# K by eight heads and a quarter of the keys, K and V in one ring: a decode step of attention beside an MLP

## The chip, the cores and the metric

The kernel runs on one core of a Trainium2 chip. The metric is the device time of one execution in microseconds (us). Before the change it is 214.77 us, the median of three runs (214.66 to 214.85). The core has five engines that run on their own and meet at semaphores: TensorE (PE, matmuls; its weight loads are shown apart as PEld), VectorE (DVE), ScalarE (ACT), GpSimd (POOL) and SyncE (SP), which here issues nearly all transfers. Sixteen DMA engines move the data.

## What is computed

One token for each of four sequences goes through two branches that are added: attention over the last 2048 keys of a cache, and an MLP behind a small mixing step.

```python
def _A_ref(x, k_cache, v_cache, wq, wo):
    W = min(4096, max(256, Sk // 4))          # 2048 of the 8192 keys
    rep = Hq // Hkv                           # 32 query heads on 16 kv heads
    q = (x @ wq).reshape(B, Sq, Hq, Dh).transpose(0, 2, 1, 3)
    k = jnp.repeat(k_cache[:, :, Sk - W:, :], rep, axis=1)
    v = jnp.repeat(v_cache[:, :, Sk - W:, :], rep, axis=1)
    scores = jnp.einsum("bhqd,bhkd->bhqk", q, k) * (Dh ** -0.5)
    p = _softmax(scores, axis=-1)
    o = jnp.einsum("bhqk,bhkd->bhqd", p, v)
    return o.transpose(0, 2, 1, 3).reshape(B, Sq, Hq * Dh) @ wo

def _B_ref(x, w1, w2, w3, w4):
    h = _gelu(_layernorm(x, axis=-1) @ w1)
...
    x1 = x + hs
    h2 = _gelu(_layernorm(x1, axis=-1) @ w3) @ w4
    return x1 + h2

xn = _layernorm(x, axis=-1)
return x + _A_ref(xn, A_k_cache, A_v_cache, A_wq, A_wo) + _B_ref(xn, B_w1, B_w2, B_w3, B_w4)
```

B is 4, D 576, F 4608, the head size Dh 128; everything is bf16. `k_cache` and `v_cache` have the shape (4, 16, 8192, 128), so a head of one sequence is 2 MB, of which the last half MB is read. Together the windows of K and V are 67 MB; the weights are 21 MB more.

## The kernel before

The program is written as a list of operations for each engine. Each has a key, and an engine's operations are sorted by it; each names the operations or counts that it waits for. A transfer is an operation of SP (line 176), so the transfers go out in the order of their keys, and one that waits holds up all behind it. All of them share one queue.

**Transfers.** First come the weights wq, w2, w1, w3 and the remainder of w3. wq, w1 and w2 lie in the V ring, w3 in `regB`, which later holds transposed keys. Then K: a unit is one kv head `g` of all four sequences, 2 MB, and lies in one of four slots of the K ring (lines 230 to 236). Partition p = 4 i + b holds the keys 64 i to 64 i + 63 of sequence b, one run of 16 KB in memory; the outer dimension of the source is i, 32 long. Units 0 to 3 wait for nothing, unit g waits until the transposes of unit g - 4 are done. V has the same layout in a ring of its own, also four slots. V0 goes after K8 (`V0_AFTER`), the rest after K15; V4 and on wait for PV of four units before. wo goes between V3 and V4 into the K ring (`WO_AFTER`, line 242). The five parts of w4 come last, into the V ring.

**Scores.** A block is eight 128x128 transposes on TensorE into one bank of PSUM (`pe_T`, line 345), with a permuted identity `perm_k` that sorts the columns by sequence, and one copy to `ktbuf` by VectorE or ScalarE (`evac`, line 355: blocks 1, 4 and 7 of eight go to ScalarE). Eight blocks are one unit. Then `pe_SC` (line 361) multiplies: 16 matmuls a unit, each with the queries of one head and one sequence as weights (32 columns, zero but for two) and 512 keys as the moving operand, into the 32 partitions of that sequence. All 16 heads add up in the same four banks, since each head's queries stand in columns of their own. The TensorE code is a hardware loop of four passes, four units each. The scores of a unit come two blocks into the next one, over the end of a pass too: a dummy unit -1 stands at the start, and the last unit's scores behind the loop.

**Softmax.** VectorE takes the maximum of each partition (`rmax`), ScalarE writes the exponentials bank by bank (L398), VectorE turns each quarter in 32x32 blocks as soon as its exponential is there (L401), TensorE permutes (L402), and VectorE makes the weights `PTg` of a unit (L412).

**Output.** `pe_PV` (line 444) is 64 matmuls a unit with the V tile as weights and 8 columns of `PTg`; VectorE normalizes the result (L456). This loop also has four passes of four units. Then a turn (L474), 64 matmuls with wo (`pe_AO`, line 465), and the products with w4 part by part (`MO0` to `MO4`, line 557): `MO0` adds into the accumulator of wo, which is then copied (L553) and folded into the final one (`pe_fold`, L543), and the other parts go straight to the final one (88 matmuls, L543). Two copies (L570, L571) and two small transfers end the kernel.

Of the kernel before, what the change touches and what calls it, by code (L numbers as in the profile page):

```python
# [6 lines left out]
BF16 = mybir.dt.bfloat16  # L7
# [5 lines left out]
NKS = 4  # L13
NVS = 4
# [3 lines left out]
NIT = 4  # L18
ACT_EVAC = (1, 4, 7)
WO_AFTER = 3  # L20
V0_AFTER = 8
# [17 lines left out]
def bass_parallel_sum__sliding_block_cached__mixer_s_mlp__decode_kernel(  # L39
# [11 lines left out]
    NHB = 8 * G  # L51
# [10 lines left out]
    with ExitStack() as ctx:  # L62
        def sb(name, shape, dt):
            return ctx.enter_context(nc.sbuf_tensor(name, shape, dt))
# [4 lines left out]
        kring_t = sb("kring", [128, NKS * UE], BF16)  # L69
        vring_t = sb("vring", [128, NVS * UE], BF16)  # L70
        W3E = 4 * F + FH
        regB_t = sb("regB", [128, max(NKT * 1024, W3E)], BF16)
        kring = kring_t[:].rearrange("p (s t d) -> p s t d", s=NKS, t=NT)
        vring = vring_t[:].rearrange("p (s t d) -> p s t d", s=NVS, t=NT)
        ktbuf = regB_t[:, 0:NKT * 1024].rearrange("p (s n) -> p s n", s=NKT)
        kttile = regB_t[:, 0:NKT * 1024].rearrange("p (t b i) -> p t b i", b=B, i=32)
        w3main = regB_t[:, 0:4 * F].rearrange("p (r n) -> p r n", r=4)
        w3rag = regB_t[:, 4 * F:W3E]
        wqmain = vring_t[:, 0:4 * Hq * Dh].rearrange("p (r n) -> p r n", r=4)
        wqrag = vring_t[:, 4 * Hq * Dh:4 * Hq * Dh + Hq * Dh // 2]  # L80
        wo_sb = kring_t[:, 0:32 * D].rearrange("p (r n) -> p r n", r=32)
        _o = 4 * Hq * Dh + Hq * Dh // 2
        w1p = vring_t[:, _o:_o + 9 * HALF]
        _o += 9 * HALF
        w2p = vring_t[:, _o:_o + 9 * HALF]
        _o += 9 * HALF
        WQ_SLOTS = -(-_o // UE)
        assert WQ_SLOTS < NVS

# [17 lines left out]
        Qs = sb("Qs", [128, 4, B, 32], BF16)  # L107
        ident_bf = sb("ident_bf", [128, 128], BF16)
        perm_k = sb("perm_k", [128, 128], BF16)
# [48 lines left out]
        for nm, cnt in (("eb", 32), ("qs", 4), ("pg", 4), ("on", 4)):  # L158
            for k in range(cnt):
                S[(nm, k)] = sem(f"{nm}{k}")  # L160
# [37 lines left out]
        P(lambda e: e.memset(Qs[:, 3], 0.0), sig=("qs", 3), key=-95.8)  # L198

        def first_counts(e):  # L200
            for k in range(NTB):
                e.sem_inc(S[("eb", 32 - NTB + k)], 1)
                e.sem_inc(S[("on", k)], 1)
        P(first_counts, key=-95.7)
        P(lambda e: e.tensor_copy(out=perm_k[:].rearrange("p (b i) -> p b i", b=B), in_=ident_bf[:].rearrange("p (i b) -> p b i", b=B)),
          waits=["ident_bf"], sig="perm_k", key=-95.5)
# [23 lines left out]
        def kv_pairs(ring_t, slot, cache, g):  # L230
            return [(ring_t[:, slot * UE:(slot + 1) * UE],
                     cache[:, g, Sk - W:Sk, :].rearrange("b (i t) d -> i b (t d)", t=NT))]

        for g in range(G):
            ev_k.append(add_dma(kv_pairs(kring_t, g % NKS, A_k_cache, g), ("k", g % NKS),
                                [f"T{8 * (g - NKS) + 7}"] if g >= NKS else [], g))
        wo_wait = f"T{8 * (G - 2) + 7}"
        for g in range(G):
            kk = KS + g if g else V0_AFTER + 0.5
            w = [f"PV{g - NVS}"] if g >= NVS else (["hT"] if g < WQ_SLOTS else [])  # L240
            ev_v.append(add_dma(kv_pairs(vring_t, g % NVS, A_v_cache, g), ("v", g % NVS), w, kk))
            if g == WO_AFTER:
                ev_wo = add_dma([(kring_t[:, 0:32 * D], A_wo.rearrange("(p r) n -> p (r n)", r=32))],
                                "wo", [wo_wait], kk + 0.1)
        w4_src = B_w4.rearrange("(p r) n -> p r n", r=RT)
        w4_sb = vring_t[:, 0:RT * D].rearrange("p (t n) -> p t n", n=D)
        for n, (t0, t1_) in enumerate(W4P):
            lst = (t1_ * D - 1) // UE
            ev_w4.append(add_dma([(w4_sb[:, t0:t1_, :], w4_src[:, t0:t1_, :])], ("w4", n),
                                 [f"PV{max(g for g in range(G) if g % NVS == lst)}"], KS + G + 0.1 * n))  # L250
# [91 lines left out]
        add("pe", pe_zeroS, waits=["zeros_bf", "perm_k", "gelu2", "gelu_h", "qT", "x1nT", "x1"], sig="zeroS", key=-1)  # L342


        def pe_T(n):
            g, k = n // 8, n % 8

            def f(e):
                ins = None
                for t in range(8):  # L350
                    ins = e.transpose(tb[n % NTB][:, t, :], kring[:, g % NKS, 8 * k + t, :], perm_k[:])  # L351
                return ins
            return f
# [7 lines left out]
        def pe_SC(g):  # L361
            def f(e):
                ins = None
                for c4 in range(4):
                    for b in range(B):
                        t0 = 8 * ((8 * g + 2 * c4) % NKT)
                        ins = e.matmul(Sps[32 * b:32 * b + 32, c4, :].rearrange("p (t i) -> p t i", t=16), lhsT=Qs[:, g % 4, b, :],  # L367
                                       rhs=kttile[:, t0:t0 + 16, b, :],
                                       start=False, stop=(g == G - 1), tile_position=(0, 32 * b), skip_group_check=True)
                return ins  # L370
            return f

        for n in range(NHB):
            p = n % 32
            w = [("L", ("k", p // 8), 16)] if p % 8 == 0 else []
            w.append(("L", ("eb", (p - NTB) % 32), 1))
            add("pe", pe_T(n), waits=w, sig=f"T{n}", key=n // 32 + 0.01 * p, loop=("k", n // 32))
            eng, f = evac(n)
            add(eng, f, waits=[f"T{n}"] + ([f"SC{n // 8 - 2}"] if n >= 8 else []), sig=("eb", p), key=n + 0.2)
        for g in range(-1, G):  # L380
            s_ = g % 4
            if g < G - 1:
                add("pe", pe_SC(g), waits=[("L", ("eb", 8 * s_ + 6), 1), ("L", ("eb", 8 * s_ + 7), 1), ("L", ("qs", s_), 1)], sig=f"SC{g}",
                    key=(g + 1) // 4 + 0.01 * (8 * ((g + 1) % 4) + 1) + 0.005, loop=("k", (g + 1) // 4))
            else:
                add("pe", pe_SC(g), waits=[("c", ("eb", 30), NIT + 1), ("c", ("eb", 31), NIT + 1), ("c", ("qs", 3), NIT + 1)],
                    sig=f"SC{g}", key=NIT + 0.5)
        for g in range(G):
            P(lambda e, g=g: e.tensor_copy(out=Qs[:, g % 4], in_=Qpad[:, g]), waits=(["qT"] if g == 0 else []) + ([f"SC{g - 4}"] if g >= 3 else []),  # L389
              sig=("qs", g % 4), key=8 * g)  # L390


        add("dve", lambda e: e.tensor_reduce(out=rmax[:], in_=Sps, axis=AX.XY, op=ALU.max), waits=[f"SC{G - 1}"], sig="rmax", key=KS)  # L393
        add("dve", lambda e: e.tensor_scalar(out=negb[:], in0=rmax[:], scalar1=-scale, scalar2=None, op0=ALU.mult),
            waits=["rmax"], sig="negb", key=KS + 0.05)
        for q in range(4):
            cs = slice(512 * q, 512 * q + 512)
            add("act", lambda e, q=q, cs=cs: e.activation(out=P_sb[:, cs], in_=Sps[:, q, :], func=ACTF.Exp, bias=negb[:, 0:1], scale=scale,  # L398
                                                          accum_out=rs4[:, q:q + 1]),
                waits=["negb"], sig=f"exp{q}", key=KS + 0.1 + 0.01 * q)  # L400
            add("dve", lambda e, cs=cs: e.transpose(PTb[:, cs], P_sb[:, cs]), waits=[f"exp{q}"], sig=f"PTb{q}", key=KS + 0.2 + 0.01 * q)  # L401
# [9 lines left out]
        for g in range(G):  # L411
            add("dve", lambda e, g=g: e.tensor_tensor(  # L412
                out=PTg[:, g % NPG], in0=PTs[:, :, 2 * g:2 * g + 2].unsqueeze(2).to_broadcast([128, NT, B, 2]),
                in1=bmask[:].unsqueeze(1).to_broadcast([128, NT, B, 2]), op=ALU.mult),
                waits=[f"PTs{q}" for q in range(4)] + ["bmask"] if g < NPG else [f"PV{g - NPG}"], sig=("pg", g % NPG),
                key=KS + 0.4 + 0.01 * g if g < NPG else KV + g - NPG + 0.6)
# [35 lines left out]
        for g in range(G):  # L452
            m = g % 4
            add("pe", pe_PV(g), waits=[("L", ("v", m), 16), ("L", ("pg", m), 1), ("L", ("on", m), 1)], sig=f"PV{g}", key=KV + g,
                loop=("v", g // 4))
# [20 lines left out]
        add("pe", pe_turn, waits=[("c", ("on", m), NIT + 1) for m in range(4)] + ["sel32"], sig="turn", key=KV + 19.9)  # L476
# [115 lines left out]
        def emit_op(eng_name, engine, op, waited, it=None):  # L592
            for w in op.waits:
                if w[0] == "L":
                    engine.wait_ge(S[w[1]], it * w[2] + w[2] if w[2] > 1 else it + 1)
                    continue
# [61 lines left out]
```

## Time and profile before

| | |
|---|---|
| runs | 214.66, 214.77, 214.85 us |
| the profiled execution | 214.71 us, of which its span is 213.5 |
| TensorE busy | 137.9 us (65% of the span), mean granted clock 0.784 |
| VectorE, ScalarE, GpSimd busy | 87.3, 59.5, 12.0 us |
| moved | 88.63 MB in 6513 packets, mean 415 GB/s |
| K unit, V unit | 2048 KB each, 16.7 and 17.6 us from issue to landing (median) |

How to read the profile: times are us from the start of the span unless marked ns. In the row of slices the span is cut into 40 parts of 5.3 us, and a digit is the busy share in tenths; the clock row has the TensorE clock that was granted, in tenths of full speed. The DMA share is a mean over the sixteen engines, and attribution at the edges lets it exceed 100% a little. The chain of waits starts at the last instruction and goes back to what released each step; in order of time each line has the start, the length and what ran. In the timeline, equal instructions are merged: start, length from the first to the last, engine, line, operation, output and inputs, count, and in brackets how long the engine sat idle before and what released it. In a table by windows each engine has its busy time and its count of instructions, followed by clock, DMA share and GB/s.

### The profile page before, as it was taken

Reading aid. Unit: us, or ns where it says so; the run is one execution under the profiler, and the core shown is the slowest. Engines: PE = TensorE matmul, PEld = TensorE weight load, DVE = VectorE, ACT = ScalarE, POOL = GpSimd, SP = SyncE. Lnnn points to the kernel's source line nnn. Section 1 sums busy time; section 2 is a strip of 40 time slices with the busy share of each in tenths; the row PEclk is TensorE's granted clock in tenths of the full one; section 3 lists DMA queues with packets and bytes.
Section 4 is the critical chain, followed back from the end, with each engine's and each line's share of the span. In section 5 each row is a group of like instructions: output and inputs, shape, how many; then the busy total and the mean of one; then the engine's idle time right before and its main releaser. Section 6 shows DMA issues by size and latency. Waiting matters only on the chain.

```text
span 213.5 us, 5829 instructions
## 1 busy us (share of the span) xinstructions
PE 137.9 (65%) x2692; PEld 108.8 (51%) x2692; DVE 87.3 (41%) x162; ACT 59.5 (28%) x72; POOL 12.0 (6%) x39
## 2 busy tenths in 40 slices
PE   0088147999999992999999818923343443333596
PEld 0036023777888881788888702923343443333444
DVE  6715203666666662266666649721111112100000
ACT  2001302665555563156665655000000000000000
POOL 8501000000000000000000000000000000000000
PEclk9999859999999998599999995555555555555569
DMA  6999989999999999999999999999999999999993
GB/s 246 430 401 498 438 363 433 433 416 421 433 430 427 421 433 433 427 424 431 430 418 439 427 436 442 424 418 430 414 430 436 424 427 430 439 411 435 426 407 129
DMA packets 6513, 88.63 MB, mean 415 GB/s; under 512 B 732, under 2 KB 872, under 8 KB 1640
## 3 DMA queue, kind: packets, MB, share of 16 engines
q1 hardware_dynamic: 6488, 88.50, 97.8%
q8 instruction: 7, 0.11, 0.2%
q10 hardware_dynamic: 16, 0.01, 0.0%
q14 instruction: 2, 0.02, 0.0%
HBM read 88.49 MB, written 0.00 MB: 415 GB/s over the span
## 4 chain that ended last, share of the span: by engine, by line
DMA 52%; PE 39%; DVE 4%; issue 2%; SPq 1%; ACT 1%
PE ps L351 23%; DMA vring<-in_A_v_cache_dram 23%; DMA regB<-in_B_w_dram 12%; DMA kring<-in_A_k_cache_dram 9%; DMA vring<-in_B_w_dram 8%; PE ps L367 7%; PE ps L448 4%; PE ps L527 2%; PE ps L543 1%; DVE PTb L401 1%; SPq L176 1%; DVE rmax L393 1%; DVE regB L359 1%; ACT PTb L537 1%; DVE PTs L409 1%
## 5 line engine op out<-in xcount | busy, mean ns | idle before, releaser
L359 DVE COPY regB<-ps 128x1024 bf16<-128x1024 bf16 x80 | 52.4, 688 | 34.0 <-PE ps L351 32.1
L351 PEld LDWEIGHTS ps<-perm_k,kring 128*128 128x128 bf16 x1024 | 58.9, 99 | 12.4 <-issue 7.8
L351 PE MATMUL ps<-perm_k,kring 128*128 128x128 bf16 x1024 | 62.4, 222 | 4.2 <-DMA kring<-in_A_k_cache_dram 4.1
L358 ACT ACTIVATE regB<-ps 128x1024 bf16<-128x1024 bf16 x48 | 47.8, 1023 | 40.6 <-PE ps L351 40.5
L448 PE MATMUL ps<-PTg,vring 128*128 128x8 bf16 x1024 | 29.5, 168 | 38.1 <-DMA vring<-in_A_v_cache_dram 36.5
L448 PEld LDWEIGHTS ps<-PTg,vring 128*128 128x128 bf16 x1024 | 28.4, 104 | 39.2 <-DMA vring<-in_A_v_cache_dram 27.5
L456 DVE TENSOR_TENSOR PTb<-ps,PTb 128x32 bf16<-128x32 f32 x16 | 3.1, 192 | 55.3 <-PE ps L448 55.2
L367 PE MATMUL ps<-regB,Qs 128*32 128x512 bf16 x272 | 18.6, 395 | 4.4 <-issue 3.1
L553 ACT ACTIVATE P_sb<-ps 100x288 f32<-100x288 f32 x1 | 0.4, 411 | 75.2 <-PE ps L463 75.2
L367 PEld LDWEIGHTS ps<-regB,Qs 128*32 128x32 bf16 x272 | 6.6, 97 | 10.6 <-issue 6.0
L412 DVE TENSOR_TENSOR PTg<-PTs,bmask 128x512 bf16<-128x512 bf16 x16 | 10.7, 682 | 0.0
L389 POOL COPY Qs<-Qpad 128x128 bf16<-128x128 bf16 x16 | 4.6, 296 | 92.0 <-PE ps L367 82.5
L527 PE MATMUL ps<-regB,x1nT 128*32 128x432 bf16 (+1 forms) x60 | 3.9, 431 | 7.1 <-DMA regB<-in_B_w_dram 7.1
L527 PEld LDWEIGHTS ps<-regB,x1nT 128*32 128x32 bf16 x60 | 1.9, 123 | 8.8 <-DMA regB<-in_B_w_dram 7.2
L540 DVE STREAM_TRANSPOSE h2T_sb<-PTb 128x1152 bf16<-128x1152 bf16 x1 | 1.4, 1379 | 12.0 <-ACT PTb L537 12.0
L402 PE MATMUL ps<-PTb,perm_p 128*128 128x512 bf16 x4 | 2.4, 608 | 4.3 <-DVE PTb L401 4.1
L293 PE MATMUL ps<-ident_bf,xn_bf 4*128 4x4 bf16 x4 | 0.3, 166 | 7.5 <-DVE ragsrc L277 7.5
L570 DVE CAST out_sb<-ps 36x144 bf16<-36x144 f32 x1 | 0.3, 300 | 9.9 <-PE ps L543 9.9
L463 PE MATMUL ps<-kring,ORT 128*4 128x288 bf16 x64 | 4.0, 443 | 0.4 <-DVE ORT L477 0.4
L315 PE MATMUL ps<-vring,xnT 128*32 128x512 bf16 x40 | 4.2, 597 | 0.0
L293 PEld LDWEIGHTS ps<-ident_bf,xn_bf 4*128 4x128 bf16 x4 | 0.2, 110 | 7.4 <-POOL ones_f L213 7.4
L537 ACT ACTIVATE PTb<-ps 128x432 bf16<-128x432 f32 (+1 forms) x3 | 1.3, 491 | 8.6 <-PE ps L527 8.6
(99 smaller groups left out, 76.9 us busy)
## 6 DMA issues: line engine op xcount, KB each, us to landing
kring<-in_A_k_cache_dram SPq DMA_DIRECT2D x16, 2048.0 KB, 16.7
vring<-in_A_v_cache_dram SPq DMA_DIRECT2D x16, 2048.0 KB, 17.6
regB<-in_B_w_dram SPq DMA_DIRECT2D x1, 4608.0 KB, 26.1
kring<-in_A_wo_dram SPq DMA_DIRECT2D x1, 4608.0 KB, 22.7
vring<-in_A_wq_dram SPq DMA_DIRECT2D x2, 2048.0 KB, 9.5
vring<-in_B_w_dram SPq DMA_DIRECT2D x2, 2016.0 KB, 17.4
vring<-in_B_w_dram SPq DMA_DIRECT2D x2, 648.0 KB, 13.7
vring<-in_B_w_dram SPq DMA_DIRECT2D x1, 720.0 KB, 14.3
```

The lines of the kernel that those rows point to most:

```text
L315: ins = e.matmul(Qps[32 * j:32 * j + 32, k, :], lhsT=x_, rhs=w, start=(r == 0), stop=(r == 4), tile_position=(0, 32 * j))
L351: ins = e.transpose(tb[n % NTB][:, t, :], kring[:, g % NKS, 8 * k + t, :], perm_k[:])
L358: return "act", lambda e: e.activation(out=ktbuf[:, n % NKT], in_=src, func=ACTF.Copy)
L359: return "dve", lambda e: e.tensor_copy(out=ktbuf[:, n % NKT], in_=src)
L367: ins = e.matmul(Sps[32 * b:32 * b + 32, c4, :].rearrange("p (t i) -> p t i", t=16), lhsT=Qs[:, g % 4, b, :], rhs=kttile[:, t0:t0 + 16, b, :],
L389: P(lambda e, g=g: e.tensor_copy(out=Qs[:, g % 4], in_=Qpad[:, g]), waits=(["qT"] if g == 0 else []) + ([f"SC{g - 4}"] if g >= 3 else []), ...
L412: add("dve", lambda e, g=g: e.tensor_tensor(out=PTg[:, g % NPG], in0=PTs[:, :, 2 * g:2 * g + 2].unsqueeze(2).to_broadcast([128, NT, B, 2]) ...
L448: ins = e.matmul(OTps(g), lhsT=vring[:, g % NVS, t, :], rhs=PTg[:, g % NPG, t].rearrange("p b e -> p (b e)"), start=(t == 0), stop=(t == N ...
L456: add("dve", lambda e, g=g: e.tensor_tensor(out=OTx[:, :, 2 * g:2 * g + 2, :], in0=OTps(g).rearrange("p (b e) -> p b e", b=B).unsqueeze(3) ...
L463: return e.matmul(ACC[h], lhsT=lhsT, rhs=rhs, start=start, stop=stop, tile_position=(k0, 32 * h))
L527: ins = e.matmul(H2ps[k][32 * j:32 * j + 32, :], lhsT=x_, rhs=w, start=(r == 0), stop=(r == 4), tile_position=(0, 32 * j))
L537: ins = e.activation(out=h2a[:, :, a:z], in_=H2ps[k].rearrange("p (i c) -> p c i", c=RT), func=ACTF.Gelu_apprx_tanh)
```

## The change

K is cut another way. A unit is now eight kv heads (every other one) of all four sequences, by a quarter of the keys: 32 rows of 128 KB, each spread over four partitions in runs of 32 KB. There are eight units of 4 MB. The outer dimension of the source is the pair of sequence and head, 32 long, with a step of two heads, 4 MiB. Units 0 to 3 are the even heads, 4 to 7 the odd ones.

K and V share one ring of 16 MB, four K slots or eight V slots. The early weights lie in it behind the first K slot, w3 too, so K unit 0 waits for nothing and units 1 to 3 wait for the last matmul of w3. `regB` holds nothing but transposed keys. V0 to V7 wait for the transposes of K units 4 to 7, V8 and on for PV eight units before. All of V follows all of K in the queue. wo goes behind V15, waiting for PV10, and the parts of w4 behind it, all waiting for PV12.

The transposes use the plain identity, and `perm_k` goes. A group of scores is 32 matmuls of 256 keys for eight blocks; the moving operand takes four neighbouring values of each transposed tile, where it was 32. The eight Q tiles of a pass are copied before it. The scores of the last eight blocks of a pass now stand at the end of that pass. The exponentials are written with strides, so that every quarter touches all of the result, and each block transpose waits for the fourth of them. Both TensorE loops have two passes instead of four, with bodies of 768 and 512 matmuls.

```diff
-NVS = 4
+NVS = 8
...
-NIT = 4
+NIT = 2
...
+    KE = 2 * UE
+    TK = 2 * NT
+    NU = 2 * NKS
+    NB = TK // 8
+    LB = NB * NKS
+    NHB = NB * NU
...
+        ring_t = sb("ring", [128, NKS * KE], BF16)
+        kring = ring_t[:].rearrange("p (s t d) -> p s t d", s=NKS, t=TK)
+        vring = ring_t[:].rearrange("p (s t d) -> p s t d", s=NVS, t=NT)
+        regB_t = sb("regB", [128, NKT * 1024], BF16)
+        kttile = regB_t[:].rearrange("p (t m x) -> p t m x", m=32, x=4)
+        _o = [KE]
+
+        def home(n):
+            _o[0] += n
+            assert _o[0] <= NKS * KE
+            return ring_t[:, _o[0] - n:_o[0]]
+        w3main = home(4 * F).rearrange("p (r n) -> p r n", r=4)
...
+        _o[0] = 0
+        wo_sb = home(32 * D).rearrange("p (r n) -> p r n", r=32)
+        WO_SLOT = (_o[0] - 1) // UE
+        w4_sb = home(RT * D).rearrange("p (t n) -> p t n", n=D)
+        W4_SLOT = (_o[0] - 1) // UE
...
-        def kv_pairs(ring_t, slot, cache, g):
-            return [(ring_t[:, slot * UE:(slot + 1) * UE],
-                     cache[:, g, Sk - W:Sk, :].rearrange("b (i t) d -> i b (t d)", t=NT))]
...
+        k_heads = A_k_cache.rearrange("b g s d -> (b g) s d")
+        for u in range(NU):
+            h, q = u // NKS, u % NKS
+            w = [k_done(u - NKS)] if u >= NKS else (["h2_4"] if u else [])
+            src = k_heads[h:B * G:2, Sk - W + 4 * TK * q:Sk - W + 4 * TK * (q + 1), :].rearrange("m (x t) d -> m x (t d)", t=TK)
+            ev_k.append(add_dma([(ring_t[:, q * KE:(q + 1) * KE], src)], ("k", q), w, u))
         for g in range(G):
+            w = [f"PV{g - NVS}"] if g >= NVS else [k_done(NU - NKS + g // 2)]
+            src = A_v_cache[:, g, Sk - W:Sk, :].rearrange("b (i t) d -> i b (t d)", t=NT)
+            ev_v.append(add_dma([(ring_t[:, (g % NVS) * UE:(g % NVS + 1) * UE], src)], ("v", g % NVS), w, KS + g))
+        ev_wo = add_dma([(wo_sb, A_wo.rearrange("(p r) n -> p r n", r=32))], "wo", [f"PV{G - NVS + WO_SLOT}"], KS + G)
...
-                                 [f"PV{max(g for g in range(G) if g % NVS == lst)}"], KS + G + 0.1 * n))
+                                 [f"PV{G - NVS + W4_SLOT}"], KS + G + 0.1 * (n + 1)))
...
-                    ins = e.transpose(tb[n % NTB][:, t, :], kring[:, g % NKS, 8 * k + t, :], perm_k[:])
+                    ins = e.transpose(tb[n % NTB][:, t, :], kring[:, u % NKS, 8 * k + t, :], ident_bf[:])
...
+                t0 = 8 * ((8 * c) % NKT)
+                for j in range(G // 2):
                     for b in range(B):
+                        ins = e.matmul(Sps[32 * b:32 * b + 32, u % NKS, 4 * NT * z:4 * NT * (z + 1)].rearrange("p (t x) -> p t x", x=4),
+                                       lhsT=Qs[:, j, b, :], rhs=kttile[:, t0:t0 + NT, 8 * b + j, :],
+                                       start=False, stop=(u >= NKS), tile_position=(0, 32 * b), skip_group_check=True)
...
+        for h in range(2):
+            for j in range(G // 2):
+                P(lambda e, h=h, j=j: e.tensor_copy(out=Qs[:, j], in_=Qpad[:, 2 * j + h]),
+                  waits=([] if j else (["qT"] if h == 0 else [f"SC{LB // 8 - 1}"])), sig=("qs", j), key=8 * h + j)
...
-            add("act", lambda e, q=q, cs=cs: e.activation(out=P_sb[:, cs], in_=Sps[:, q, :], func=ACTF.Exp, bias=negb[:, 0:1], scale=scale,
+            add("act", lambda e, q=q: e.activation(out=P_sb[:].rearrange("p (t q x z) -> p q z t x", q=4, x=4, z=2)[:, q],
+                                                   in_=Sps[:, q, :].rearrange("p (z t x) -> p z t x", z=2, x=4), func=ACTF.Exp, bias=negb[:, 0:1], scale=scale,
...
-            add("dve", lambda e, cs=cs: e.transpose(PTb[:, cs], P_sb[:, cs]), waits=[f"exp{q}"], sig=f"PTb{q}", key=KS + 0.2 + 0.01 * q)
+            add("dve", lambda e, cs=cs: e.transpose(PTb[:, cs], P_sb[:, cs]), waits=["exp3"], sig=f"PTb{q}", key=KS + 0.2 + 0.01 * q)
```

More of the change, by code (lines that the diff above doesn't have):

```diff
@@ L17 @@
 NTB = 4
-NIT = 4
+NIT = 2
 ACT_EVAC = (1, 4, 7)
-WO_AFTER = 3
-V0_AFTER = 8
 FOLD = 14
@@ L238, in bass_parallel_sum__sliding_block_cached__mixer_s_mlp__decode_kernel, with k_done @@
[L238 to L244, printed above, removed]
+        def k_done(u):
+            return f"T{NB * u + NB - 1}"
@@ L378, in bass_parallel_sum__sliding_block_cached__mixer_s_mlp__decode_kernel @@
             eng, f = evac(n)
[L379 to L387, printed above, removed]
@@ L594, in emit_op @@
                 if w[0] == "L":
-                    engine.wait_ge(S[w[1]], it * w[2] + w[2] if w[2] > 1 else it + 1)
+                    engine.wait_ge(S[w[1]], it * w[2] + w[2] if w[2] > 1 else it + 1 + sum(w[3:]))
                     continue
```

87 lines of the change are left out of this document (32 added, 55 removed).

## The prediction

> **What bounds the kernel now.** I read the slices of the span first, then the DMA queues, then the chain of waits in order of time, then matmul rows where the chain touches TensorE.
>
> ```profile
> span 213.5 us, 5829 instructions
> ...
> PEclk9999859999999998599999995555555555555569
> DMA  6999989999999999999999999999999999999993
> ...
> q1 hardware_dynamic: 6488, 88.50, 97.8%
> q8 instruction: 7, 0.11, 0.2%
> ```
>
> The transfer engines are busy at 90% or more in every slice but the first, one early one and the last: 97.8% of the span on the one queue that carries the caches and weights. No engine can shorten the kernel unless those bytes move faster, or the pieces before the first and behind the last byte shrink. The same chain of waits says what happens at the end.
>
> ```profile
> 190.93 17.48 DMA vring<-in_B_w_dram
> ...
> 208.46 3.13 PE ps L543 x88
> 211.61 0.30 DVE out_sb L570
> ```
>
> The second large piece of w4 lands at 208.41, 88 matmuls follow, then the copy and the output transfer, 1.9 us from 211.59 to the end of the span. Between the pieces TensorE hardly waits: it is on the path for the last 3.1 us, and nearly nowhere else.
>
> **The packets.** Two stretches of the transfer view, 19 to 27 us (the 36 KB runs of w3) and 150 to 190 us (the 16 KB runs of V), give the price of a run.
>
> ```profile
> DMA packets 96, 3.52 MB, mean 440 GB/s; under 512 B 0, under 2 KB 0, under 8 KB 0
> ...
> q1 hardware_dynamic: 95, 3.50, 101.6%
> ```
>
> ```profile
> DMA packets 1172, 17.11 MB, mean 428 GB/s; under 512 B 128, under 2 KB 128, under 8 KB 128
> ...
> q1 hardware_dynamic: 1172, 17.11, 100.5%
> ```
>
> The first: 8 us x 16 engines x 1.016 / 95 = 1369 ns for 36.86 KB (3.50 MB / 95). The second: 40 x 16 x 1.005 / 1044 (1172 less 128 completion marks) = 616 ns for 16.38 KB. The line through both is 13.7 ns a packet and 36.8 ns a KB, so a 32.77 KB run should take 1218 ns against 2 x 616. K is 16 x 128 = 2048 packets now, 128 on each engine, 78.8 us; afterwards 64 x 1218 = 78.0 us. Gain **0.87 us**. Its ends: nothing, if a 32 KB run is cut in two or both rates come from something else, and 0.96 us, if 32 KB already runs at the bytes per ns of 36 KB. I take 0.87, as the 36 KB row shows that such a run stays one packet.
>
> Against it stands code. The TensorE loop bodies grow from 320 to 768 matmuls (K) and from 256 to 512 (V), and 16 behind the loop go. Unrolled once, the program before has 2692 - 3 x 320 - 3 x 256 = 964 matmuls for 7 fetches; 688 more make 5 more fetches. Seven cost 0.2% of 213.5 us, 0.061 us each: **0.31 us** more. (No fetch, 0; a second fetch of both bodies, 1280 matmuls, 9 more, 0.9 us. The passes after the first show none now, so I take 0.31.) Net on the transfers: -0.56 us.
>
> **Do the transfers stay fed?** This is where the new ring can lose. K unit 0 goes without a wait, units 1 to 3 wait for the last w3 matmul.
>
> ```profile
> 3.68 26.07 DMA regB<-in_B_w_dram
> ...
> 29.79 3.92 PE ps L527 x45
> ...
> 36.19 1.06 PE ps L351 x16
> ```
>
> ```profile
> regB<-in_B_w_dram SPq DMA_DIRECT2D x1, 576.0 KB, 27.0
> ```
>
> The w3 remainder, issued half a us behind the main part (3.68), lands 27.0 us after its issue, at 31.2; unit 0 then takes 8 x 1.218 = 9.7 us, to 40.9. The w3 matmuls end at 33.7, so units 1 to 3 are issued 7 us before the queue is empty. Cost nothing, covered by unit 0. K flows to 31.2 + 78.0 = 109.2, V0 to V7 to 109.2 + 64 x 0.616 = 148.6. V0 to V7 wait for transposes of units 4 to 7, which follow their landing by about one unit. V8 waits for PV0, and SP holds everything behind it: V9 to V15, wo, w4. So the date of PV0 is the one to work out.
>
> ```profile
> 85.08 1.89 PE L351 MATMUL ps<-perm_k,kring 128*128 128x128 bf16 x16 [4.12 <-DMA kring<-in_A_k_cache_dram]
> 86.90 1.90 PE L367 MATMUL ps<-regB,Qs 128*32 128x512 bf16 x16
> 88.73 4.56 PE L351 MATMUL ps<-perm_k,kring 128*128 128x128 bf16 x64
> 93.53 1.05 PE L367 MATMUL ps<-regB,Qs 128*32 128x512 bf16 x16 [0.24 <-issue]
> 94.51 3.77 PE L351 MATMUL ps<-perm_k,kring 128*128 128x128 bf16 x64
> ...
> 99.50 3.69 PE L351 MATMUL ps<-perm_k,kring 128*128 128x128 bf16 x63
> ```
>
> 64 transposes with their scores take 99.50 - 94.51 = 4.99 us, 16 times: 79.8. K can start only at about 41.2 instead of 36.2, after an idle stretch like the 4.12 us one shown, which cost another 2.5 us at half clock (85.08 to 93.53 against 5.9). A loop now ends on its own last scores, which wait for the last evacuation: twice about 2 us, as the one such stop shows (119.48 + 2.85, scores first at 123.49). Last scores end: 41.2 + 79.8 + 2.5 + 4 = 127.5.
>
> ```profile
> 119.48 2.85 PE L351 MATMUL ps<-perm_k,kring 128*128 128x128 bf16 x48
> 123.49 1.05 PE L367 MATMUL ps<-regB,Qs 128*32 128x512 bf16 x16 [1.16 <-DVE regB L359]
> ...
> 133.04 5.67 PE L448 MATMUL ps<-PTg,vring 128*128 128x8 bf16 x206
> ...
> 198.81 1.87 PE L448 MATMUL ps<-PTg,vring 128*128 128x8 bf16 x64 [3.02 <-DMA vring<-in_A_v_cache_dram]
> ```
>
> ```profile
> 127.10 0.69 ACT L398 ACTIVATE P_sb<-ps,negb 128x512 bf16<-128x512 f32 x1 [2.41 <-DVE negb L394]
> ...
> 127.91 2.72 DVE L401 STREAM_TRANSPOSE PTb<-P_sb 128x512 bf16<-128x512 bf16 x4 [0.85 <-ACT P_sb L398]
> ...
> 129.10 0.69 ACT L398 ACTIVATE P_sb<-ps,negb 128x512 bf16<-128x512 f32 x1
> ```
>
> From the last scores to PV0 were 8.5 us (124.54 to 133.04). The block transposes now wait for the fourth exponential, not the first: 129.10 - 127.10 = 2.0 us later. PV0 ends at 127.5 + 8.5 + 2.0 + 1.9 = 139.9. V8 is wanted at 148.6 less the time from an issue to its bytes: a **margin of about 7 us** (an estimate from these rows). It hides all of this, and the permutation copy dropped on POOL, the eight Q copies between the passes (0.3 us each, under ten blocks of transposes) and the strided exponential (were it twice as long, +2.8 us).
>
> No row shows the new score matmuls: 512 instead of 272, half as long, their moving operand in runs of 4 values instead of 32. The columns are the same, so the near row is 1.05 us a group. Low end 0.94: PV issues 64 pairs in 1.87 us, 29 ns each, x 32. High end: the half-clock group, 1.90 us. I take 1.18 (31 x 29 ns and the 0.27 us tail of a 256-column matmul): +0.13 x 16 = 2 us inside the margin. From 1.05 + 7 / 16 = 1.49 us it decides.
>
> **The end.** wo moves from the middle to a place between V15 and w4. w4 is 5.3 MB, 12.4 us at 428 GB/s; the last bytes stay where they are, so wo lands where V15 does now, 198.8 - 0.6 = 198.2, and V15 eleven us earlier. Now PV15, the turn, wo's matmuls and the first w4 part run back to back:
>
> ```profile
> 201.81 4.01 PE L463 MATMUL ps<-kring,ORT 128*4 128x288 bf16 x64 [0.38 <-DVE ORT L477]
> 205.61 1.45 PE L463 MATMUL ps<-vring,h2T_sb 128*4 128x288 bf16 x28
> 207.58 0.66 PE L543 MATMUL ps<-P_sb,sel_h 100*4 100x144 f32 x8 [0.52 <-ACT P_sb L553]
> 208.46 3.11 PE L543 MATMUL ps<-vring,h2T_sb 128*4 128x144 bf16 x88 [0.21 <-DMA vring<-in_B_w_dram]
> ```
>
> ```profile
> 84.10:87.50 3.40, 2.42 (x24) 1.92 (x28) 0.69 (x1) 0.50 (x1) 0.00 (x0) 0.50 0.98 419
> 87.50:90.90 3.40, 3.40 (x41) 2.33 (x30) 0.97 (x2) 0.53 (x1) 0.30 (x1) 0.57 1.03 439
> ...
> 200.20:203.60 3.40, 2.54 (x55) 1.66 (x55) 0.48 (x2) 0.00 (x0) 0.00 (x0) 0.50 0.95 403
> 203.60:207.00 3.40, 3.40 (x68) 1.84 (x56) 0.00 (x0) 0.00 (x0) 0.00 (x0) 0.58 1.00 423
> 207.00:210.40 3.40, 2.67 (x76) 2.21 (x73) 0.00 (x0) 0.41 (x1) 0.00 (x0) 1.00 0.78 308
> ```
>
> The granted clock (third column from the right; before it busy time and count of PE, weight loads, DVE, ACT, POOL) is 0.50 all through V. It came back at 207.0 after a stretch of 3.4 us that was full of matmuls; a stretch that was busy for 2.42 or 2.54 of 3.4 us did not bring it. The last 88 matmuls thus ran at full clock, 35 ns each. Afterwards the dense 5.2 us are torn: wo's matmuls 198.2 to 202.2, w4's first part (lands 203.0) to 204.5, the fold to 205.7, a gap to 207.85. Only if the 3.4 us grid falls well does wo's 4.0 us fill a stretch, and then the clock must last through the gaps. At half clock the 88 cost what wo's 64 did, with 288 columns on four strips for 144 on two: 62.7 ns each, 5.5 us for 3.1. The clock can return under way (a full stretch after 207.85 ends 210.6 at the earliest); for that I take off 0.5. So matmuls end at 207.85 + 0.05 + 5.0 = 212.9, where 211.59 - 0.56 = 211.03 would have been due: **+1.9 us**.
>
> The Trainium skill, "TensorE: Matmul & The Clock Gate", Part 1, says the same of the cause: the clock opens after one busy window of about 3.4 us and closes after an idle one. The trace agrees (3.40 of 3.40 us opened it). By that rule alone, 4.0 dense us hold a whole window in about one case of six, by my rows somewhat more often.
>
> **Sum**, against the profiled execution's own 214.71 us (213.5 of span and 1.2 around it; the median 214.77 is 0.06 above): 214.71 - 0.87 + 0.31 + 1.9 = **216.0 us**. Its own range is 215.0 (clock soon back) to 216.7 (never, 214.15 + 2.5).
>
> **Rivals.**
> *The clock opens in time* (chance 0.28): the end is bound by w4 as now, 214.71 - 0.56 = 214.15 us. For it: the torn stretch still holds 4.0 dense us and no row shows at what share between 2.54 and 3.4 the gate opens. Against: one gap of 0.8 and one of 2.1 us.
> *The heads collide* (0.25), the side on which the change loses most. Now 16 engines read rows 16 KB apart; afterwards they read sixteen heads at the same place of each, 4 MB apart. If those accesses queue at one part of the memory, K flows slower, and every us goes to the end.
>
> ```profile
> 1.20:2.40 1.20, 0.00 (x0) 0.00 (x0) 0.49 (x3) 0.99 (x1) 1.12 (x4) 1.00 0.80 168
> 2.40:3.60 1.20, 0.00 (x0) 0.00 (x0) 1.20 (x4) 0.29 (x1) 1.20 (x3) 1.00 0.70 273
> ```
>
> The only slow stretches of the trace are the first: 273 GB/s at 0.70 busy, 390 a full share, which on K's 78 us is 78 x (427/390 - 1) = +7.4: 221.6 us at full clock, 223.4 at half. The very first packets, 168 / 0.80 = 210, would be +80 us; they are start-up, and I leave that end outside. It decides as soon as a K packet exceeds 1232 ns.
> The Trainium skill, "DMA: Bandwidth & Descriptors", section "Latency and other measured facts", has copies with a row pitch of 4 or 8 MiB at 103 GB/s where other pitches give 207 to 214; by that the sum would be about 293 us. No trace here shows such a pitch, the rows there were 16 KB, and here each head is read 128 KB on end, which lets engines drift apart.
> *Scores are slow* (0.10): at 1.90 us a group PV0 ends 16 x 0.85 = 13.6 us later, V8 stalls the queue by 13.6 - 7 = 6.6: 220.8 us.
> *32 KB runs are no cheaper* (0.05): 214.71 + 0.31 + 1.9 = 216.9, or 215.0 with the clock.
>
> **How the numbers follow.** The forecast has 0.32. The range 213.7 to 224 holds it, its bounds, all rivals at the prices of rows, and leaves out the far part of the colliding heads and little below: about 0.17. A measurement of this kernel tells 0.2%, 0.43 us. Faster (below 214.3) is nearly only the first rival: 0.27. Same (to 215.2): its weak cases and an early clock: 0.13. Slower: 0.60.
>
> **What would show it.** Packets: K's stretch should have 1218 ns a packet and 430 GB/s or more; 1240 or more is collision. Queue: DMA above 90% in all slices from the second to the last but one; a dip near 148 us is V8. Scores: 1.1 to 1.3 us a group of 32. End: the row of 88 matmuls 5.0 us instead of 3.11, with clock 0.50 at 207 us. I am wrong if that row stays near 3.1 us, or if any gap opens in K.

## The result, and the profile after

The changed kernel takes 223.84 us (median of five runs, 223.43 to 225.41), the one before 214.77: a ratio of 1.0436, 95% interval 1.0419 to 1.0452. That is slower, as forecast, but by 9.1 us where 1.3 were forecast. The profiled execution is the longest of the five, 225.41 us, with a span of 224.2 and a mean granted clock of 0.749, where the other four have 0.770 to 0.778.

The same slices and queues as before, from the page of the changed kernel:

```profile
span 224.2 us, 6286 instructions
...
PEclk9999758569999999999999965555555555555556
DMA  6999899999999999999999999999999999999950
GB/s 241 430 441 477 361 448 345 380 330 428 383 389 383 433 389 418 403 439 393 439 401 433 433 424 436 421 427 427 424 427 433 424 427 430 465 414 412 417 206 6
...
q1 hardware_dynamic: 5336, 88.49, 95.6%
q8 instruction: 13, 0.21, 0.4%
```

From the sixth slice on the transfer engines are as busy as before, so nothing starves them. But from the seventh slice to the twentieth, where K flows, they move 330 to 439 GB/s, where the kernel before has a steady 416 to 433:

```profile
GB/s 246 430 401 498 438 363 433 433 416 421 433 430 427 421 433 433 427 424 431 430 418 439 427 436 442 424 418 430 414 430 436 424 427 430 439 411 435 426 407 129
```

The packets say it plainly. The transfer view of the changed kernel from 40 to 100 us, where only K flows:

```profile
DMA packets 831, 23.96 MB, mean 399 GB/s; under 512 B 96, under 2 KB 96, under 8 KB 96
...
q1 hardware_dynamic: 824, 23.86, 99.9%
```

60 us x 16 engines x 0.999 / (824 - 96) = 1317 ns a packet (the 96 small packets are completion marks). The forecast had 1218. Over the 64 packets of each engine that is 6.3 us.

The end of the chain of waits, and the matmuls there:

```profile
183.87 32.91 DMA ring<-in_B_w_dram
...
216.83 5.46 PE ps L544 x88
...
222.31 0.30 DVE out_sb L571
```

```profile
198.64 0.27 PE L475 MATMUL ps<-sel,PTb 128*128 128x32 bf16 x4 [0.48 <-DVE PTb L457]
207.30 4.01 PE L464 MATMUL ps<-ring,ORT 128*4 128x288 bf16 x64 [8.39 <-DMA ring<-in_A_wo_dram]
212.03 1.85 PE L464 MATMUL ps<-ring,h2T_sb 128*4 128x288 bf16 x28 [0.72 <-DMA ring<-in_B_w_dram]
214.40 1.13 PE L544 MATMUL ps<-P_sb,sel_h 100*4 100x144 f32 x8 [0.52 <-ACT P_sb L554]
216.83 5.44 PE L544 MATMUL ps<-ring,h2T_sb 128*4 128x144 bf16 x88 [1.30 <-DMA ring<-in_B_w_dram]
```

The second large part of w4 lands 8.4 us later than before (216.8 against 208.4), and the 88 matmuls behind it take 5.44 us instead of 3.11, at a clock of 0.50, as the prediction had it. 8.4 + 2.3 are the 10.7 us of this execution. The higher mean clock of the other four means that theirs was up for some 9 to 13 us more (an estimate: the difference times 224 us, over the half that a closed clock takes); so the 2.3 us hold for this execution, and not for the median.

### The profile page after: what moved, and what is told of

Read it like the earlier page. It is cut to its first block, busy times and chain, and to the rows that moved or that the text cites. A ratio compares the mean times of both kernels' runs of the same rounds, so it can differ in the third digit from the quotient of the medians.

```text
span 224.2 us, 6286 instructions
## 1 busy us (share of the span) xinstructions
PE 141.2 (63%) x2932; PEld 118.8 (53%) x2932; DVE 87.0 (39%) x162; ACT 60.0 (27%) x72; POOL 11.0 (5%) x37
## 4 chain that ended last, share of the span: by engine, by line
DMA 57%; PE 29%; ACT 6%; issue 3%; DVE 3%; SPq 2%
DMA ring<-in_B_w_dram 26%; DMA ring<-in_A_k_cache_dram 18%; PE ps L350 14%; DMA ring<-in_A_v_cache_dram 12%; PE ps L368 5%; PE ps L449 5%; ACT regB L357 4%; PE ps L544 2%; PE ps L528 2%; SPq L182 2%; ACT P_sb L398 1%; DVE PTb L402 1%; DVE rmax L393 1%; DVE PTs L410 1%; PE ps L425 0%
## 5 line engine op out<-in xcount | busy, mean ns | idle before, releaser
L350 PE MATMUL ps<-ident_bf,ring 128*128 128x128 bf16 x1024 | 63.2, 224 | 7.1 <-DMA ring<-in_A_k_cache_dram 7.1
L350 PEld LDWEIGHTS ps<-ident_bf,ring 128*128 128x128 bf16 x1024 | 60.0, 100 | 11.2 <-issue 9.2
L449 PE MATMUL ps<-PTg,ring 128*128 128x8 bf16 x1024 | 29.2, 168 | 29.0 <-DMA ring<-in_A_v_cache_dram 21.7
L449 PEld LDWEIGHTS ps<-PTg,ring 128*128 128x128 bf16 x1024 | 28.3, 104 | 30.0 <-DMA ring<-in_A_v_cache_dram 21.6
L368 PE MATMUL ps<-regB,Qs 128*32 128x256 bf16 x512 | 17.1, 272 | 5.9 <-ACT regB L357 5.4
L368 PEld LDWEIGHTS ps<-regB,Qs 128*32 128x32 bf16 x512 | 12.9, 94 | 8.4 <-issue 5.4
L413 DVE TENSOR_TENSOR PTg<-PTs,bmask 128x512 bf16<-128x512 bf16 x16 | 10.7, 682 | 0.0
L528 PE MATMUL ps<-ring,x1nT 128*32 128x432 bf16 (+1 forms) x60 | 5.0, 524 | 7.4 <-DMA ring<-in_B_w_dram 7.4
L464 PE MATMUL ps<-ring,ORT 128*4 128x288 bf16 x64 | 4.0, 442 | 8.4 <-DMA ring<-in_A_wo_dram 8.4
L544 PE MATMUL ps<-ring,h2T_sb 128*4 128x144 bf16 x88 | 5.4, 323 | 1.3 <-DMA ring<-in_B_w_dram 1.3
L544 PEld LDWEIGHTS ps<-ring,h2T_sb 128*4 128x4 bf16 x88 | 5.1, 125 | 1.9 <-DMA ring<-in_B_w_dram 1.9
```

The lines of the kernel that those rows point to most:

```text
L350: ins = e.transpose(tb[n % NTB][:, t, :], kring[:, u % NKS, 8 * k + t, :], ident_bf[:])
L368: ins = e.matmul(Sps[32 * b:32 * b + 32, u % NKS, 4 * NT * z:4 * NT * (z + 1)].rearrange("p (t x) -> p t x", x=4), lhsT=Qs[:, j, b, :], rh ...
L413: add("dve", lambda e, g=g: e.tensor_tensor(out=PTg[:, g % NPG], in0=PTs[:, :, 2 * g:2 * g + 2].unsqueeze(2).to_broadcast([128, NT, B, 2]) ...
L449: ins = e.matmul(OTps(g), lhsT=vring[:, g % NVS, t, :], rhs=PTg[:, g % NPG, t].rearrange("p b e -> p (b e)"), start=(t == 0), stop=(t == N ...
L464: return e.matmul(ACC[h], lhsT=lhsT, rhs=rhs, start=start, stop=stop, tile_position=(k0, 32 * h))
L528: ins = e.matmul(H2ps[k][32 * j:32 * j + 32, :], lhsT=x_, rhs=w, start=(r == 0), stop=(r == 4), tile_position=(0, 32 * j))
```

## The experiments

Two theories for the slow packets: *colliding heads* (the engines read the same place of many heads, 4 MiB apart, and queue in memory) and *long runs* (a run of 32 KB is served unevenly, wherever it lies). For the rest of the loss: the *clock* at the end, and the *code fetches*. Each kernel was timed beside the kernel before on the same chip; the medians of that one were 214.75 to 214.87 us.

**The step between heads.** Three kernels change only where K's 32 rows lie.

```diff
-            src = k_heads[h:B * G:2, Sk - W + 4 * TK * q:Sk - W + 4 * TK * (q + 1), :].rearrange("m (x t) d -> m x (t d)", t=TK)
+            src = bass.AP(tensor=A_k_cache.tensor, offset=(h * Sk + Sk - W + 4 * TK * q) * Dh,
+                          ap=[[2 * Sk * Dh - 65536, 2 * B * G // 4], [UE * 2, 4], [1, UE * 2]])
```

> The changed kernel, with one number of K's source changed: the step from one head to the next is 4 MiB less 128 KiB, so that the 32 rows lie at 32 different places of a 4 MiB period. Runs stay 32 KB, units 4 MB, waits as they were; the keys read are partly others, so the output is not the reference's. Theory of the colliding heads: K's packets go back to 1213 to 1220 ns in the mean (1319 in the changed kernel), the end of the transfers moves back by 6 to 8 us, and the time is 216 to 218 us, with the matmuls of the end still at half clock. Rival, long runs (a 32 KB run is served unevenly wherever it lies): packets stay at 1300 or more, 223 to 225 us.

> As the kernel with 128 KiB taken off the step, but with only 4 KiB taken off: 32 rows spread over 128 KB. If the heads collide through equal address bits above 4 KiB, this cures most of it: 216 to 219 us, packets 1213 to 1240 ns. If they collide because the windows that the engines read overlap in the 4 MiB period at all, little is cured: 221 to 224 us. Long runs: 223 to 225 us.

 (2048 elements in place of 65536.)

> The changed kernel with K's 32 rows taken from 32 consecutive heads, step 2 MiB instead of 4 MiB; the place of a head in the batch is then another than the scores assume, so the output is not the reference's. If what collides is equal address bits up to 4 MiB, half of the engines now differ in one more bit: mean packet 1225 to 1290 ns, 217.5 to 221.5 us. If only the common place within a head counts, all is as with 4 MiB: 1300 to 1340 ns, 223 to 225.5 us.

 (`k_heads[32 * h:32 * h + 32, ...]`.)

Measured: 217.07 us with 128 KiB off the step (ratio to before 1.0114, 1.009 to 1.0137), 216.99 with 4 KiB (1.0116, 1.0086 to 1.0146), 217.29 with 2 MiB (1.0105, 1.0083 to 1.0128). The transfer view of the first, again from 40 to 100 us:

```profile
DMA packets 888, 25.80 MB, mean 430 GB/s; under 512 B 97, under 2 KB 97, under 8 KB 97
...
q1 hardware_dynamic: 881, 25.69, 99.8%
```

and of the one with 2 MiB:

```profile
DMA packets 889, 25.83 MB, mean 430 GB/s; under 512 B 97, under 2 KB 97, under 8 KB 97
...
q1 hardware_dynamic: 882, 25.72, 99.9%
```

Both give 1222 ns a packet (60 x 16 x 0.998 / 784), 4 ns from the price that the prediction read off the 16 and 36 KB runs; the kernel with 4 KiB has 1221. The long run is innocent, the step is guilty, and 4 KiB off the 4 MiB cure it. So does half the step: for 2 MiB a part of the loss or all of it was expected, and there was none.

**The same step with short runs.** The kernel before, with K read as 32 heads at 4 MiB, in its own runs of 16 KB:

```diff
-            ev_k.append(add_dma(kv_pairs(kring_t, g % NKS, A_k_cache, g), ("k", g % NKS),
+            o = Sk - W + 4 * NT * (g % 8)
+            src = A_k_cache.rearrange("b g s d -> (b g) s d")[g // 8:B * G:2, o:o + 4 * NT, :].rearrange("m (x t) d -> m x (t d)", t=NT)
+            ev_k.append(add_dma([(kring_t[:, (g % NKS) * UE:(g % NKS + 1) * UE], src)], ("k", g % NKS),
...
```

> The kernel before, with K's units read as 32 heads at a step of 4 MiB, four runs of 16 KB from each; all else as before. The scores are then formed from other keys, so the output is not the reference's. Theory of the colliding heads: the same loss without any long run, K's packets 650 to 670 ns in the mean instead of 616, 219 to 223 us. Rival, long runs: 214.5 to 215.2 us.

Measured: 238.07 us (235.78 to 242.58), ratio 1.1046 (1.099 to 1.1101). The direction is that of the colliding heads, the size about three to five times what I expected (23 us for 4 to 8). The profiled execution is the longest of the four, 242.58 us. Its transfer view from 40 to 60 us, and that of the kernel before:

```profile
DMA packets 438, 6.38 MB, mean 319 GB/s; under 512 B 48, under 2 KB 48, under 8 KB 48
...
q1 hardware_dynamic: 435, 6.34, 101.4%
```

```profile
DMA packets 577, 8.45 MB, mean 422 GB/s; under 512 B 61, under 2 KB 61, under 8 KB 61
...
q1 hardware_dynamic: 573, 8.39, 99.1%
```

838 ns a packet (20 x 16 x 1.014 / 387) against 619 (20 x 16 x 0.991 / 512). Over the 128 packets of an engine the 23 us of the median are some 180 ns a packet (an estimate, if all of the loss is in K), so this longest execution overstates the loss a little. Here each head is read 64 KB on end and then left, in the changed kernel 128 KB. Engines that start in step and drift apart while they read on would explain why the shorter stay costs more. But no run here tests the drift, and the start of K speaks against its plain form, for the first packets are not the slow ones. In the trace the first 48 packets of K take 616 ns in the mean, the 65th to the 96th 1208. In a table by windows, 4.8 us from about the start of K in this kernel (the last column is GB/s):

```profile
29.00:31.40 2.40, 1.65 (x20) 0.78 (x24) 0.00 (x0) 0.00 (x0) 0.00 (x0) 0.50 1.06 442
31.40:33.80 2.40, 2.40 (x36) 1.28 (x32) 0.00 (x0) 0.00 (x0) 0.00 (x0) 0.50 1.08 246
```

The kernel before moves 428 and 423 GB/s in the same stretches.

**The clock at the end.** 53 matmuls that nobody reads are put into the gaps of TensorE, first into the changed kernel as it is.

```diff
+        def pe_warm(n):
...
+                    ins = e.matmul(ps[:, 4, 64:512], lhsT=ident_bf[:], rhs=PTs[:, 0:14, :].rearrange("p t r -> p (t r)"), start=True, stop=True)
...
+        add("pe", pe_warm(30), waits=["ORT"], sig="warm0", key=KV + 19.95)
+        add("pe", pe_warm(10), sig="warm1", key=KV + 20.05)
+        add("pe", pe_warm(13), sig="warm2", key=KT + 20.6)
```

> The changed kernel with 53 matmuls added whose result nobody reads, in the three gaps of TensorE at the end: 30 ahead of the product with wo, 10 behind it, 13 behind the fold. Theory of the clock: the granted clock is 1.0 when the second large part of w4 lands, the last 88 matmuls take 3.0 to 3.3 us instead of 5.4, and the time falls by 2.0 to 2.4 us, to 221.4 to 221.9. Rival: the end is set by the last part of w4, not by the matmuls; then the time falls by 0 to 1 us.

Measured: 224.17 us (223.63 to 225.68), no gain on 223.84, so neither expectation came out. Its matmuls at the end:

```profile
214.99 2.63 PE L483 MATMUL ps<-PTs,ident_bf 128*128 128x448 bf16 x13
217.66 3.08 PE L554 MATMUL ps<-ring,h2T_sb 128*4 128x144 bf16 x88
```

The clock did what it should, 3.08 us for the 88. But the runs of both kernels lie 2 us apart among themselves, as the collisions move the last transfers, so this pair cannot show a gain of 2 us. I repeated it where the collisions are gone:

> The changed kernel with the step between heads 128 KiB short of 4 MiB (other keys are read, so the output is not the reference's), and the 53 unread matmuls in the three gaps of TensorE at the end. With the collisions gone, the second large part of w4 lands at 209.5 us as without the added matmuls. Theory of the clock: the last 88 matmuls then take 3.1 us instead of 4.4 and the time is 215.6 to 216.1. Rival: the last small parts of w4, on the slowest transfer engine, set the end anyway; then 216.7 to 217.1.

Measured: 215.71 us (215.62 to 215.9), 1.36 less than the 217.07 without the added matmuls; ratio to before 1.0045 (1.0032 to 1.0057). The end without them, and with them:

```profile
199.98 4.01 PE L465 MATMUL ps<-ring,ORT 128*4 128x288 bf16 x64 [8.41 <-DMA ring<-in_A_wo_dram]
204.72 1.52 PE L465 MATMUL ps<-ring,h2T_sb 128*4 128x288 bf16 x28 [0.72 <-DMA ring<-in_B_w_dram]
206.76 0.66 PE L545 MATMUL ps<-P_sb,sel_h 100*4 100x144 f32 x8 [0.52 <-ACT P_sb L555]
209.54 4.36 PE L545 MATMUL ps<-ring,h2T_sb 128*4 128x144 bf16 x88 [2.12 <-DMA ring<-in_B_w_dram]
```

```profile
209.52 3.18 PE L555 MATMUL ps<-ring,h2T_sb 128*4 128x144 bf16 x88
```

Both start at 209.5; 4.36 against 3.18 us is the whole difference of these two executions, 217.03 and 215.83 us. The theory of the clock holds where the heads do not collide.

**The longer loops alone.** The kernel before with both TensorE loops in two passes of eight units; the waits count on by a half pass.

```diff
-NIT = 4
+NIT = 2
...
-            add("pe", pe_T(n), waits=w, sig=f"T{n}", key=n // 32 + 0.01 * p, loop=("k", n // 32))
+            add("pe", pe_T(n), waits=w, sig=f"T{n}", key=n // 64 + 0.01 * (n % 64), loop=("k", n // 64))
...
-                loop=("v", g // 4))
+                loop=("v", g // 8))
...
-                    engine.wait_ge(S[w[1]], it * w[2] + w[2] if w[2] > 1 else it + 1)
+                    engine.wait_ge(S[w[1]], it * (2 * w[2]) + w[2] * (w[3] + 1))
```

> The kernel before with both TensorE loops in two passes of eight units instead of four passes of four; nothing else. 12 or 13 code fetches instead of 7. Theory of the single engine: each fetch of 16 KB holds up one of the sixteen transfer engines by 1.5 us, nothing evens that out before the end, and with more than eight or so fetches some engine has two: the last part of w4 lands 1.2 to 1.8 us later, 216.0 to 216.6. Rival, the price of the prediction: fetches cost their share of sixteen engines, 0.06 us each: 215.0 to 215.2.

Measured: 216.22 us (216.19 to 216.45), ratio 1.007 (1.0057 to 1.0083): +1.47 us for five more fetches, where their share of sixteen engines would be 0.3. The last 9.5 us of the transfer view, first the kernel before, then this one (40 slices of 0.24 us each, a digit is the mean share of the sixteen engines):

```profile
DMA  7969769697797995899997644444100000000000
```

```profile
DMA  9497997979798895655555314111100000000000
```

Each span's end is at the right edge. Before, the engines stop in two steps: more than half of them near digit 22, the rest, near 4 tenths, run five or six slices, 1.3 us, longer. In the other there are three steps, the last of 1 tenth, and the engines that finish first do so that much sooner before the end. The two traces have the landing of every engine: the second large part of w4 lands on the sixteen between 206.62 and 208.41 us before, and in the longer code on thirteen between 206.56 and 208.42 and on three between 209.78 and 209.93. Those three set the landing, 1.52 us later. The work is the same: the packets of q1 take 97.8% of 213.5 us before and 97.2% of 214.9 us here, 208.8 and 208.9 us. So it is the spread over the engines that costs, and nothing evens it out before the end. The instruction queue of the longer code:

```profile
q8 instruction: 12, 0.20, 0.4%
```

**Another cut of K.** Heads u and u + 8 of all sequences, all keys, 32 KB runs; the outer dimension of the source is 16 pieces of keys:

```diff
+            src = k_heads[u:B * G:NU, Sk - W:Sk, :].rearrange("m (i t) d -> i m (t d)", t=TK)
...
+                for y in range(2):
+                    for j in range(2):
+                        for b in range(B):
+                            ins = e.matmul(Sps[32 * b:32 * b + 32, 2 * z + y, :].rearrange("p (t i) -> p t i", i=16),
...
```

> The changed kernel with another cut of K: a unit is heads u and u + 8 of all sequences with all keys, still 4 MB in runs of 32 KB, but the outer dimension of the source is now 16 pieces of keys at a step of 32 KB, so that the engines read side by side in one head. The scores are 16 matmuls of 512 keys for eight blocks again, with a permuted identity. Theory of the colliding heads: packets of 1213 to 1225 ns in the mean, 216.5 to 217.3 us. Rival, long runs in a unit of 4 MB: 222 us or more.

> The same with the 53 unread matmuls at the end. Theory of the clock: 215.4 to 216.1 us, and what is left above 214.8 is code fetches on the slowest engine. Rival: no gain from the clock, 216.5 to 217.3.

Measured: 298.55 and 297.24 us (ratios 1.3887, 1.3842 to 1.3932, and 1.3883, 1.3818 to 1.3948). All expectations missed; long runs, put at 222 us or more, had already run at full price above. The transfer view of the first, 40 to 100 us:

```profile
DMA packets 436, 12.64 MB, mean 211 GB/s; under 512 B 48, under 2 KB 48, under 8 KB 48
...
q1 hardware_dynamic: 432, 12.58, 99.4%
```

Half the rate, 2485 ns a packet. A kernel with the engines again 32 KB apart, but an outer dimension of 32, tells whether that is memory or the shape:

```diff
+            src = A_k_cache[:, u, Sk - 2 * W:Sk, :].rearrange("b (i t) d -> i b (t d)", t=TK)
```

> The changed kernel with a unit of K made of one head of all sequences and 4096 keys: outer dimension 32 at a step of 32 KB, four rows 32 MiB apart on each, runs of 32 KB (other keys than the scores assume, so the output is not the reference's). It tells apart why the unit of two heads, outer dimension 16 at the same step of 32 KB, ran at half rate. If engines that read 32 KB apart collide in memory: packets near 2500 ns again, 295 to 300 us. If it was the outer dimension of 16, by which an engine writes eight neighbouring partitions instead of two groups of four: packets of 1213 to 1230 ns, 216.7 to 217.5 us.

Measured: 217.49 us (217.0 to 217.81), ratio 1.0128 (1.011 to 1.0146):

```profile
DMA packets 892, 25.93 MB, mean 432 GB/s; under 512 B 97, under 2 KB 97, under 8 KB 97
...
q1 hardware_dynamic: 885, 25.82, 100.3%
```

Full rate at the same distance in memory, 1222 ns a packet. The distance of 32 KB is cleared. What is left is the outer dimension of 16, the eight rows per piece that go with it (four here), and the distance between those rows, 16 MiB there and 32 MiB here. No run tells these three apart, so the cause of the half rate stays open.

## Why the prediction was right or wrong

**What bounds it.** Right: the transfers bind, before and after, and every us that they lose is at the end.

**The packets.** The price of a run was right and the run was not: 1222 ns with the heads out of step, against 1218 read from the rows, but 1317 in the changed kernel. This is the step that failed, by the prediction's own sign (1240 ns or more is collision). It took the price from rows in which neighbouring engines read neighbouring addresses, and applied it to an access that no row showed. The first rival on the slow side, colliding heads, had the mechanism: 7.4 us there, 6.8 measured (223.84 - 217.07). That the sizes are near is luck, since the 7.4 came from a slow stretch at the start of the trace, where no heads are read. The rival got 0.25 where it was the main effect. Its loss is also uneven: in the profiled execution fifteen engines have their share of the second large part of w4 between 211.6 and 214.9 us, and the last at 216.8.

The rule of the Trainium skill ("DMA: Bandwidth & Descriptors", "Latency and other measured facts") was the evidence for the rival, and I discounted it because the trace did not show such a pitch and because engines might drift apart, which the start of K does not bear out. Its row, on copies between two tensors in memory, has 103 GB/s at a pitch of 4 MiB, 207 at 512 KiB, 214 with 4 KiB added to the 4 MiB, and also 164 at 2 MiB, which the prediction left out when it gave other pitches 207 to 214. These runs agree that the step is what matters and that 4 KiB, here taken off, restore the rate. With the sizes they do not agree: half the rate there, 399 against 430 GB/s here, 319 against 422 with short runs, and nothing at 2 MiB. What the row gives as the mechanism it calls an inference itself, and no run here shows it.

**The code.** The fetches were counted well (5 more expected, 6 seen) and priced wrongly, the second term that failed: 0.31 us as a share of sixteen engines, 1.47 us measured for five, since the slowest engine sets each landing. The gain of the runs, 128 x 616 - 64 x 1222 ns = 0.6 us, is thus less than the longer loops cost. The code's extra 1.16 us is about what the kernel without collisions, 217.07 us, has above the 216.0 forecast: slower than before would have been right without the heads, too.

**The feeding of the queue.** Right. Unit 0 covered units 1 to 3, and V8 did not stall: the share stays above 90% from the sixth slice to the last but two. The dates were worked out well: with 128 KiB off the step, where K flows at the forecast price, the last scores end at 127.0 and PV0 at 139.5 us, against 127.5 and 139.9 forecast. The rival of slow scores is refuted; the row of the changed kernel has 1.06 us for 32 matmuls with runs of four values, where I took 1.18:

```profile
55.58 1.06 PE L368 MATMUL ps<-regB,Qs 128*32 128x256 bf16 x32 [0.29 <-ACT regB L357]
```

**The end.** Right in mechanism: wo lands 8.4 us after the turn, the dense stretch is torn, the clock is 0.50 for the 88 matmuls. The forecast had +1.9 us; 2.3 in the profiled execution, 1.36 in the medians once the collisions are gone. The 88 matmuls were to take 5.0 us; they take 5.44 in the profile of the changed kernel, and 4.36 to 5.16 in the four whose packets run at full price without added matmuls. The rival that the clock opens in time was half right in these four. There it did open, in three of them for the whole first part of w4 (28 matmuls in 1.03 us), and closed again in the gap. With 2 MiB:

```profile
199.92 4.01 PE L464 MATMUL ps<-ring,ORT 128*4 128x288 bf16 x64 [8.40 <-DMA ring<-in_A_wo_dram]
204.64 1.03 PE L464 MATMUL ps<-ring,h2T_sb 128*4 128x288 bf16 x28 [0.71 <-DMA ring<-in_B_w_dram]
206.19 0.66 PE L544 MATMUL ps<-P_sb,sel_h 100*4 100x144 f32 x8 [0.52 <-ACT P_sb L554]
209.47 5.16 PE L544 MATMUL ps<-ring,h2T_sb 128*4 128x144 bf16 x88 [2.63 <-DMA ring<-in_B_w_dram]
```

The prediction gave wo's matmuls about one case in six, or somewhat more, to open the clock, since they would have to fill a whole stretch of the clock's grid. They need not. In these traces the clock changes only at whole multiples of 3.41 us, and it came back after such stretches with 3.39 us of matmuls (2 MiB, 200.54 to 203.95), 3.33 (one head a unit), 3.17 (4 KiB off) and 2.70 (128 KiB off). In the changed kernel 2.69 us did not bring it (209.13 to 212.54).

**The account.** Colliding heads +6.77, clock +1.36, code +1.47, longer runs -0.64: +8.96 us, and 9.07 were measured. The first three are differences of medians, the last is worked out from packets. A part of it can be checked: with the collisions and the clock's loss gone, 215.71 us are 0.96 above the kernel before, and code and runs give 0.83. But the clock's term was measured without collisions; in the changed kernel itself the added matmuls gained nothing, so that the terms add up there is argued, not shown.

**What stays open.** What part of the memory the heads share at 4 MiB and not at 2; why the short runs lose three times as much; why the load with an outer dimension of 16 runs at half the rate. No version beats the kernel before: 215.71 us, with other keys, a step that does not collide and the clock held up, is the nearest, and by the account the longer code is what keeps it behind.

## What to carry to other kernels

A packet price read from one access pattern holds for that pattern: before a source is cut another way, look at which addresses the sixteen engines read at the same moment, and try another distance before trusting the price: here 4 MiB lost, 4 KiB less did not, and 2 MiB, a power of two as well, did not either. In a kernel whose transfers are busy from end to end, every addition to the slowest engine counts in full, code fetches too, so a longer loop body has a price even where TensorE does not bind. And a gap ahead of the last matmuls has a price of its own when the clock of TensorE falls in it, or does not rise before it: in the two executions shown side by side, the last matmuls took 1.2 us more.

## What the runs showed of the hardware that was not expected

Sixteen engines reading 32 rows at a step of 4 MiB moved 399 GB/s in runs of 32 KB and 319 in runs of 16 KB. At steps of 2 MiB, 4 MiB less 4 KiB and 4 MiB less 128 KiB, runs of 32 KB moved 430 to 431, and runs of 16 KB that lie 16 KB apart 422. A load of 4 MB into 128 partitions with an outer dimension of 16 in its source ran at 211 GB/s, one with 32 at 432, with all engines busy in both. Five code fetches more, of 16 KB each, made a kernel 1.47 us longer that is bound by its transfers. In the twelve traces, cut from the first recorded change of the clock on into the stretches of 3.41 us at whose ends it changes, full clock followed on every stretch at half clock with 2.71 us or more of matmuls and on none with less than 2.60. The stretches of PV's 8-column matmuls are the exception: up to 3.41 us busy, they never brought it. From full clock it fell after every stretch with less than 1.50 us of matmuls and held after every one with more than 1.70. And a moving operand in runs of four bf16 values went as fast as one in runs of 32: 1.06 us for the same columns, against 1.05.
